# Later chunks: the values of the last two batches, between the fourth up quarter's products and its 64-row rest, in the accumulators' free columns set to zero

## The chip, the cores and the metric

The kernel runs on one core of one Trainium2 chip. The metric is device time in microseconds (us). The core has five engines that run their own instruction streams and wait for one another by semaphores: TensorE (PE; its weight loads are listed as PEld), VectorE (DVE), ScalarE (ACT), GpSimd (POOL) and SyncE (SP), whose queue here issues nearly all DMAs. Matmuls write to PSUM, which has eight banks of 512 float32 columns on 128 partitions.

## The reference

An mLSTM cell over 4 batches, 8 heads, 768 steps and head size 40 is followed by a feed-forward block with exact GELU on 3072 tokens (320 features, 2048 hidden). Cut to what matters:

```
for t in range(S):
    m_new = max(f[t] + m, i[t])
    C = exp(f[t] + m - m_new) * C + exp(i[t] - m_new) * outer(v[t], k[t])
    n = exp(f[t] + m - m_new) * n + exp(i[t] - m_new) * k[t]
    y[t] = sigmoid(o[t]) * (C @ q[t]) / max(abs(n @ q[t]), 1)
x = y as (tokens, heads * head size)
out = gelu(x @ w_in) @ w_out
```

## The kernel before

The sequence is cut into six chunks of 128 steps. In a chunk the cell is computed in parallel form: scores k q, masked and weighted by W, times the values v, plus what the state from earlier chunks gives ("far"). The feed-forward block of a chunk c runs on TensorE while the cell of chunk c + 1 is computed in between, so that each later chunk (1 to 5) is one long list of steps. Float32 accuracy comes from splitting each operand: x into x_hi, x_rest and x_low, the hidden values g into three parts, the weights into two, so each product is three passes.

The order of the steps is written out by hand in strings: SECOND for chunk 1, LATER for chunks 2 to 4, LAST for chunk 5. A word is a letter with its number, and each engine gets its instructions in the order of the words. A word that concerns one engine only can stand anywhere between words of other engines without a change. The words that matter here:

- U q, u q: the four up quarters. U is the products with K = 128 (24 matmuls of 512 columns, L966), u its rest with the last 64 rows of x (12 matmuls on half the array, L977). Quarter 0 writes the four banks called main, quarters 1 to 3 the four banks called side. side and main each are two pools with two banks; they change places from chunk to chunk. In a quarter the first 12 matmuls of U fill the two banks of the first pool, the other 12 those of the second.
- g n: gelu of one of 16 hidden blocks on ACT (L984), its first part on ACT (L985), the two others on DVE (L986, L987). The whole value lies in a tile with the tag "sig", of which there are two.
- d n: the down products of block n (L991, 12 matmuls of 320 columns) into the four accumulators po in main. An accumulator takes 320 of the 512 columns of its bank; the free ones are called beside.
- C b, h b: for the batches b and b + 1 the state is read (read_two, L621), then the update's products are made (L632), far is scaled on DVE (L639), the state is decayed on POOL (L643) and added to on DVE (L647). Both use two banks of side, called pf.
- S b: the scores of two batches (L568), in all four banks of side; DVE multiplies them into W (L574).
- V b: the values of one batch (later_values, L674, 32 small matmuls for a batch, two records each), added to far on DVE (L678). Batches 0 and 1 go to beside, 2 and 3 to a bank of side.
- Y b, t b, X b, R b: the output gate and the division on DVE (L685 to L690), a copy on ACT, the transposes on PE (L708) into a bank px of side, and the split into the parts of x on ACT (L718) and DVE (L727, L728).
- E t: the accumulators of the chunk before are copied to o_sb on ACT (L1015), two to a tile of the tag "o_sb", of which there are two, and sent by SP in two halves each (L859).
- K, Q: transposes of k and q on DVE (L512). D: values times a decay on POOL. M: masking of W on POOL (L474). W: its exponentials on ACT (L500). G: the output gate's tanh on ACT.
- L, B, J, O and +: loads and copies by SP's queue: blocks of k and q, M for W, k and v, the output gate, and copies of k and q in DRAM for later chunks.

In the code before, far has two buffers of its own (tag "hs"). far of batches 0 and 1 takes them in h0; when these batches are through X, far of batches 2 and 3 takes them in h2.

Of the kernel before, what the change touches and what calls it, by code (L numbers as in the profile page):

```python
# [9 lines left out]
F32 = mybir.dt.float32  # L10
# [4 lines left out]
OP = mybir.AluOpType  # L15

P = 128
# [18 lines left out]
for at, first, key in ((HI_AT, 10, "h0"), (LO_AT, 10, "h1"), (HI_AT, 13, "b0"), (LO_AT, 13, "b1"), (HI_AT, 0, "b2"), (LO_AT, 0, "b3")):  # L36
    at.update((first + i, (key, i)) for i in range(3))
LATER = """
 U0 u0 E0 E1 E2 E3 K1 Q1 L2 D0 D1 C0 h0 M2 M3 g0 g1 g2 g3 +
 U1 u1 g4 d0 g5 d1 g6 d2 g7 S0 d3 K2 Q2 L3 W2 W3 G0 G1 G2 G3 +  # L40
 U2 V0 V1 u2 g8 d4 g9 K3 Q3 B4 B5 J0 J1 d5 g10 d6 g11 S2 L4 d7
 U3 u3 + M4 M5 Y0 Y1 D2 D3 K4 W4 W5 g12 t0 d8 g13 t1 d9 g14 X0 X1 R0 d10 g15 R1 C2 h2 O0 O1 d11 V2 V3 Y2 t2 B6 J2 d12 Y3 t3 Q4 L5 B7 d13 X2 X3 R2 d14 R3 d15 + O2 O3"""

SECOND = """
 U0 u0 j2 o0 o1 K1 Q1 L2 M0 M1 D0 D1 W0 W1 a0,3 b0,3 a3 b3 a4,2 b4,2 a6,2 b6,2 C0 h0 M2 M3 g0 g1 g2 g3 o2 o3 + +
 U1 u1 Z Z Z g4 d0 g5 d1 g6 d2 g7 S0 d3 K2 Q2 L3 W2 W3 G0 G1 G2 G3 Z Z +
 U2 V0 V1 u2 + g8 d4 g9 K3 Q3 B4 B5 J0 J1 d5 g10 d6 g11 S2 L4 d7
 U3 u3 + M4 M5 Y0 Y1 D2 D3 K4 W4 W5 g12 t0 d8 g13 t1 d9 g14 X0 X1 R0 d10 g15 R1 C2 h2 O0 O1 d11 V2 V3 Y2 t2 B6 J2 d12 Y3 t3 Q4 L5 B7 d13 X2 X3 R2 d14 R3 d15 + O2 O3"""

LAST = """  # L50
 U0 u0 E0 E1 E2 E3 g0 g1 g2 g3 U1 u1 g4 d0 g5 d1 g6 d2 g7 d3 
# [5 lines left out]
def kernel(  # L57
# [16 lines left out]
    nc = tc.nc  # L74

    B, H, S, D = q.shape
    L = P
    NCH = S // L
    NP = H // 2
    D1 = D + 1  # L80
    DP = 64
    BH = B * H
    DM = H * D
    DFF = moe_w_in.shape[1]
    NF = DFF // P
    TG = B * L
# [13 lines left out]
    raw = ctx.enter_context(tc.tile_pool(name="raw", bufs=2))  # L100
    two = ctx.enter_context(tc.tile_pool(name="two", bufs=2))
    outp = ctx.enter_context(tc.tile_pool(name="outp", bufs=2))
    dram = ctx.enter_context(tc.tile_pool(name="dram", bufs=1, space=bass.MemoryType.DRAM))
    ps_tr = ctx.enter_context(tc.tile_pool(name="ps_tr", bufs=2, space=bass.MemoryType.PSUM))
    ps_h = ctx.enter_context(tc.tile_pool(name="ps_h", bufs=2, space=bass.MemoryType.PSUM))
    ps_mm = ctx.enter_context(tc.tile_pool(name="ps_mm", bufs=2, space=bass.MemoryType.PSUM))
# [25 lines left out]
    vb = [const.tile([P, H, D1], F32, name=f"vb{n}", tag=f"vb{n}") for n in range(NQ)]  # L132
# [29 lines left out]
    def load(n, first=0, end=4):  # L162

        if n >= NCH * B:
            return
        c, b = divmod(n, B)
        for src, dst in ((q, qb), (k, kb), (v, vb), (o_gate, None))[first:end]:
            if dst is kb and c > 1:
                dst = k_later
            if dst and swapped(c, b):  # L170
                x, to = src[b, :, c * L:(c + 1) * L, :].rearrange("h p d -> p h d"), dst[turn_of(n)][:, :, 0:D]
                for i in range(2):
                    nc.sync.dma_start(out=to[halves[i]], in_=x[halves[1 - i]])
                continue
            nc.sync.dma_start(out=dst[turn_of(n)][:, :, 0:D] if dst else out_of(n),
                              in_=src[b, :, c * L:(c + 1) * L, :].rearrange("h p d -> p h d"))
# [19 lines left out]
    def turn_of(n):  # L196

        return n % NLD if n < 2 * B else (n - 2 * B) % NQ
# [184 lines left out]
    bits, sig, pow2 = {}, {}, {}  # L383
# [46 lines left out]
    def unread(bank):  # L430
        for _ in range(idle[0]):
            nc.tensor.matmul(bank, ident, ident, start=True, stop=True, skip_group_check=True)
        idle[0] = 0

    def per_head(t, c, b):
        return t[:, c, b * H:(b + 1) * H].unsqueeze(2)
# [5 lines left out]
    def by_set(px):  # L442

        return px.rearrange("p k (a i) -> p (k a) i", a=2)

    def in_place(x, b):

        return x.rearrange("p k (a t) -> p (k a) t", a=2)[:, :, b * R:(b + 1) * R]
# [9 lines left out]
    class Cell:  # L458
# [153 lines left out]
        def read_two(self, b0):  # L612

            c, two_b = self.c, (b0, b0 + 1)
            banks = self.banks = [self.side[1][0].tile([P, H + NP, D1], F32, name="pf", tag=self.side[1][1]) for _ in range(2)]
            for i, b in enumerate(two_b):
                qT = self.qT[b]
                for p in range(NP):
                    for r in halves:
                        for hip in range(2):  # L620
                            nc.tensor.matmul(banks[hip][r, NP * i + p, :], qT[halves[hip], p, r],  # L621
                                             state[b][halves[hip], p, 0:D1], start=True, stop=True)

        def update_two(self, b0):

            c, two_b, banks = self.c, (b0, b0 + 1), self.banks
            if c + 1 < NCH:
                for i, b in enumerate(two_b):
                    vw = self.vw.pop(b)
                    for p in range(NP):  # L630
                        for hip in range(2):
                            nc.tensor.matmul(banks[i][used[hip], H + p, :], k_later[turn_of(c * B + b)][:, 2 * p + hip, :],  # L632
                                             vw[:, 2 * p + hip, :], start=True, stop=True)
            add = []
            for i, b in enumerate(two_b):
                self.far[b] = fars[0].tile([P, H, D1], F32, name="far", tag="hs", bufs=2)
                by_hip = lambda t, hip: t.rearrange("p (m two) d -> p m two d", two=2)[:, :, hip, :]
                for hip in range(2):
                    nc.vector.tensor_tensor(out=by_hip(self.far[b], hip), in0=banks[hip][:, NP * i:NP * i + NP, :],  # L639
                                            in1=by_hip(per_head(gT, c - 1, b), hip).to_broadcast([P, NP, D1]), op=OP.mult)  # L640
                if c + 1 < NCH:
                    st, d = state[b][:, :, 0:D1], dec[:, c - 1, b * NP:(b + 1) * NP].unsqueeze(2).to_broadcast([P, NP, D1])
                    nc.gpsimd.tensor_tensor(out=st, in0=st, in1=d, op=OP.mult)  # L643
                    for r in used:
                        add.append((st[r], banks[i][r, H:H + NP, :]))
            for st, to in add:
                nc.vector.tensor_tensor(out=st, in0=st, in1=to, op=OP.add)  # L647

# [11 lines left out]

        def later_values(self, b):

            n, hs = self.c * B + b, self.far.pop(b)
            Pm = W.pop(n)
            by_hip = lambda t: [t.rearrange("p (m two) d -> p m two d", two=2)[:, :, hip, :] for hip in range(2)]
            if b < 2:
                ph = beside[2 * b:2 * b + 2]
            else:
                whole = self.side[0][0].tile([P, H, D1], F32, name="ph", tag=self.side[0][1])
                ph = by_hip(whole)  # L670
            for hip in range(2):
                for p in range(NP):
                    for r in quarters:
                        nc.tensor.matmul(ph[hip][r, p, :], Pm[:, 2 * p + hip, r], vb[turn_of(n)][:, 2 * p + hip, :], start=b > 1,  # L674
                                         stop=True, skip_group_check=b < 2)
            self.hs[b] = hs
            for to, x in zip(by_hip(hs), ph) if b < 2 else ((hs, whole),):
                nc.vector.tensor_tensor(out=to, in0=x, in1=to, op=OP.add)  # L678

        def finish(self, b):  # L680
            n, hs = self.c * B + b, self.hs.pop(b)
# [18 lines left out]

        def turn_y(self, b):
            n, t = self.c * B + b, slice(b * L, (b + 1) * L)
            pool, tag = self.side[b // 2] if self.c > 1 else (ps_tr, "tr") if self.c > 0 else (ps_mm, "b")
            px = pool.tile([P, NX + 1, L], F32, name="px", tag=tag)
            unread(px[:, 0, :])
            for k in range(NX + 1):
                y = ob[n % NLD][:, k * P:(k + 1) * P] if k < NX else self.rest.get(b, y_rest).rearrange("p two r -> p (two r)")
                nc.tensor.transpose(px[:, k, :], y, ident)  # L708
            self.turned.append(b)
            if self.c < 2 and len(self.finished) > len(self.turned):  # L710
                self.twice(b + 1)
            if self.c == 0:
                nc.scalar.copy(out=first_x[:, :, t], in_=px)
                return
            self.px[b] = px
            if "x" not in parts:
                parts["x"] = raw.tile([P, NX + 1, TG], F32R, name="x_hi", tag="x", bufs=1)
            nc.scalar.activation(out=in_place(parts["x"], b), in_=by_set(px), func=AF.Copy, scale=PART)  # L718
            if self.c == 1 and b < 2:
                load(n + NLD, 1, 3)  # L720
# [12 lines left out]
    parts, fars, w_hi, w_lo, beside = {}, [], {}, {}, []  # L733
# [304 lines left out]
    def first_blocks():  # L1038
# [3 lines left out]
        for r in (32, 96):  # L1042
# [8 lines left out]
                 d=lambda: decays_last(0, 1), q=lambda: decays_last(1, NCH - 1), r=halves_out, p=halves_back,  # L1051
# [56 lines left out]
```

## Time and profile before

| | us |
|---|---|
| median of 3 runs | 438.81 |
| lowest and highest of them | 438.38, 438.86 |
| the profiled execution, its own time | 438.46 |
| its span | 436.7 |
| granted TensorE clock | 1.0 |

The profile follows one execution. Its page gives the busy time of each engine; the chain of waits is the chain of work that ended last, followed back from the last instruction; the timeline gives each engine's instructions in order of time. Where a row has "[idle before <-releaser]", the engine stood idle for that long, and what is named ended it. The rows of the SyncE queue (SPq) are issues of DMAs; "to landing" counts from an issue until the data has arrived. The page's groups for the work around the change, with count, busy time and mean of one:

```profile
L986 DVE TENSOR_TENSOR g_parts<-g_whole,g_parts 128x512 fp32r<-128x512 f32 x80 | 57.0, 713 | 58.1 <-ACT g_parts L985 56.0
L984 ACT ACTIVATE g_whole<-pu 128x512 f32<-128x512 f32 x80 | 47.1, 589 | 74.2 <-PE pu L977 63.7
L574 DVE TENSOR_TENSOR W<-ps,W 128x256 f32<-128x256 f32 (+1 forms) x48 | 17.7, 414 | 4.2 <-PE ps L568 3.2
out_dram<-o_sb SPq DMA_DIRECT2D x36, 80.0 KB, 2.0
```

### The profile page before, as it was taken

The numbers are of one execution on the slowest core, as the hardware profiler recorded it, in microseconds if no ns is written. First come the engines' busy times: TensorE is split into PE (matmuls) and PEld (weight loads), VectorE is DVE, ScalarE is ACT, GpSimd is POOL, SyncE is SP. The second block draws the span as 40 slices with busy tenths as digits, with TensorE's granted clock in tenths as the row PEclk, the third lists the DMA queues.
The fourth block names the chain that finished last, engine by engine and source line by source line (L and its number), as shares of the span: only waits on it lengthen the run. The fifth ranks groups of instructions, "written<-read, shape, count | busy, mean of one in ns | idle before, by whom it ended". The sixth has DMA issues, their size and how long they took to land.

```text
span 436.7 us, 13291 instructions
## 1 busy us (share of the span) xinstructions
PE 427.3 (98%) x5472; PEld 374.6 (86%) x5472; DVE 296.0 (68%) x680; ACT 277.3 (63%) x595; POOL 48.8 (11%) x77
## 2 busy tenths in 40 slices
PE   8989999999999999999999999999999999999996
PEld 7777888877988899988899988899988889979986
DVE  8797687797888697747597747597746586533330
ACT  4989999856889985228785229785247715243441
POOL 3001030000430041030041030040010000000000
PEclk9999999999999999999999999999999999999999
DMA  7999994577791592662492653571561400010001
GB/s 151 220 214 243 233 256 87 138 211 179 229 154 56 106 176 60 115 179 50 84 187 42 123 158 60 117 134 32 110 156 17 62 2 2 22 42 2 1 2 60
DMA packets 162268, 48.83 MB, mean 112 GB/s; under 512 B 147776, under 2 KB 155232, under 8 KB 162208
## 3 DMA queue, kind: packets, MB, share of 16 engines
q1 hardware_dynamic: 161888, 47.65, 50.1%
q8 instruction: 43, 0.70, 0.6%
q10 hardware_dynamic: 320, 0.33, 0.2%
q14 instruction: 17, 0.14, 0.1%
HBM read 43.84 MB, written 9.37 MB: 122 GB/s over the span
## 4 chain that ended last, share of the span: by engine, by line
PE 73%; DVE 2%; ACT 2%; DMA 1%; issue 1%; ACTq 0%
PE po L991 31%; PE pu L966 24%; PE pu L977 7%; PE ps L568 3%; PE pf L621 2%; PE ph L674 1%; PE po L888 1%; PE po L674 1%; PE px L708 1%; DMA bits<-in_moe_w_out_dram 1%; PE pf L632 1%; DVE pow L416 1%; DVE w_out L419 0%; ACT w_out_part L935 0%; ACT g_part L873 0%
## 5 line engine op out<-in xcount | busy, mean ns | idle before, releaser
L991 PE MATMUL po<-w_out_part,g_parts 128*128 128x320 f32 x960 | 140.7, 303 | 0.0
L991 PEld LDWEIGHTS po<-w_out_part,g_parts 128*128 128x128 f32 x960 | 131.6, 189 | 5.9 <-issue 4.6
L986 DVE TENSOR_TENSOR g_parts<-g_whole,g_parts 128x512 fp32r<-128x512 f32 x80 | 57.0, 713 | 58.1 <-ACT g_parts L985 56.0
L984 ACT ACTIVATE g_whole<-pu 128x512 f32<-128x512 f32 x80 | 47.1, 589 | 74.2 <-PE pu L977 63.7
L985 ACT ACTIVATE g_parts<-g_whole 128x512 fp32r<-128x512 f32 x80 | 50.5, 631 | 8.3 <-PE po L991 5.1
L474 POOL TENSOR_SCALAR_AFFINE_SELECT W<-W 128x1024 f32<-128x1024 f32 (+2 forms) x20 | 21.7, 1088 | 189.2 <-DMA W<-M_d 154.4
L500 ACT ACTIVATE W<-W,aT 128x128 f32<-128x128 f32 x128 | 38.8, 389 | 0.3
L987 DVE CAST g_parts<-g_whole 128x512 fp32r<-128x512 f32 x80 | 36.2, 453 | 0.0
L699 ACT COPY far<-ob 128x128 f32<-128x128 f32 x16 | 4.6, 290 | 32.9 <-DVE ob L690 32.9
L966 PE MATMUL pu<-x_hi,w_in_hi 128*128 128x512 f32 x80 | 24.2, 384 | 0.0
L966 PE MATMUL pu<-x_hi,hi_first 128*128 128x512 f32 x80 | 24.0, 381 | 0.1
L966 PE MATMUL pu<-x_rest,hi_first 128*128 128x512 f32 x80 | 23.8, 379 | 0.0
L966 PE MATMUL pu<-x_rest,w_in_hi 128*128 128x512 f32 x80 | 23.8, 379 | 0.0
L966 PE MATMUL pu<-x_low,w_in_lo 128*128 128x512 f32 x80 | 23.8, 379 | 0.0
L966 PE MATMUL pu<-x_low,w_in 128*128 128x512 f32 x80 | 23.8, 379 | 0.0
L888 PE MATMUL po<-w_out,g 128*128 128x320 f32 x80 | 22.0, 432 | 0.0
L404 ACT ACTIVATE sig<-bits 128x320 f32<-128x320 f32 (+1 forms) x26 | 15.2, 586 | 10.4 <-issue 6.1
L574 DVE TENSOR_TENSOR W<-ps,W 128x256 f32<-128x256 f32 (+1 forms) x48 | 17.7, 414 | 4.2 <-PE ps L568 3.2
L888 PEld LDWEIGHTS po<-w_out,g 128*128 128x128 f32 x80 | 15.0, 190 | 5.9
L639 DVE TENSOR_TENSOR far<-pf,gT 128x164 f32<-128x164 f32 x32 | 8.4, 319 | 16.1 <-PE pf L632 11.7
L416 DVE SCALAR_TENSOR_TENSOR pow<-sig,pow 128x320 uint32<-128x320 uint32 (+1 forms) x26 | 15.4, 592 | 4.3 <-ACT pow L405 4.3
L1015 ACT ACTIVATE o_sb<-po 128x320 f32<-128x320 f32 x20 | 7.5, 443 | 16.7 <-PE po L991 16.7
(196 smaller groups left out, 778.9 us busy)
## 6 DMA issues: line engine op xcount, KB each, us to landing
W<-M_d SPq DMA_DIRECT2D x16, 512.0 KB, 6.5
bits<-in_moe_w_in_dram SPq DMA_DIRECT2D x20, 256.0 KB, 4.2
bits<-in_moe_w_out_dram SPq DMA_DIRECT2D x16, 320.0 KB, 4.6
blocks<-kq_d SPq DMA_DIRECT2D x32, 128.0 KB, 3.5
ob<-in_o_gate_dram SPq DMA_DIRECT2D x24, 160.0 KB, 4.1
out_dram<-o_sb SPq DMA_DIRECT2D x36, 80.0 KB, 2.0
wide<-M_d SPq DMA_DIRECT2D x4, 512.0 KB, 4.8
kq_d<-in_k_dram SPq DMA_DIRECT2D x6, 320.0 KB, 4.6
```

The source lines that it names most:

```text
L416: nc.vector.scalar_tensor_tensor(out=p, in0=s, scalar=3, in1=p, op0=OP.logical_shift_left, op1=OP.bitwise_or)
L474: nc.gpsimd.affine_select(out=x, in_=x, compare_op=OP.is_ge, fill=1.0e30, base=base, pattern=[[0, H], [1, x.shape[2]]], channel_multiplier=-1)
L500: nc.scalar.activation(out=W[n][:, h, :], in_=src, func=AF.Exp, scale=-1.0, bias=aT[:, self.c, r:r + 1])
L574: nc.vector.tensor_tensor(out=w[r, :, t], in0=ps[i][hip][r, :, t], in1=w[r, :, t], op=OP.mult)
L888: nc.tensor.matmul(to, xs[k][:, b * L:(b + 1) * L], w, start=(n == 0 and k == 0), stop=(n == NF - 1 and k + 1 == len(xs)), skip_group_chec ...
L966: nc.tensor.matmul(in_pairs(pus[i][e]), w3(at[k])[n][:, e, i * P:(i + 1) * P], in_turns(x3[n][:, k, :]), start=(n == 0 and k == 0), stop=F ...
L977: nc.tensor.matmul(in_pairs(pus[i][e]), w3(r)[n][h, p % 2, i * P:(i + 1) * P], in_turns(x3[n][h, NX, :]), start=False, stop=(n == 2), skip ...
L984: nc.scalar.activation(out=whole, in_=self.pus[n // 4][n % 4 // 2][n % 2], func=AF.Gelu)
L985: nc.scalar.activation(out=hi, in_=whole, func=AF.Copy, scale=PART)
L986: nc.vector.tensor_tensor(out=rest, in0=whole, in1=hi, op=OP.subtract)
L987: nc.vector.tensor_copy(out=low, in_=whole)
L991: nc.tensor.matmul(in_pairs(self.po[t]), x[:, t * L:(t + 1) * L], in_turns(w), start=(n == 0 and k == 0), stop=(n == NF - 1 and k == 2), s ...
```

## The change

The order of the steps changes in LATER, and in SECOND from the third up quarter on. TensorE's order in a later chunk is, with the down products:

```
before  U0 u0 C0 h0 U1 u1 d0-d2 S0 d3 U2 V0 V1 u2 d4-d6 S2 d7 U3 u3 d8 d9 X0 X1 d10 C2 h2 d11 V2 V3 d12 d13 X2 X3 d14 d15
after   U0 C0 u0 h0 U1 u1 d0-d2 S0 d3 U2 V0 V1 u2 d4-d6 S2 d7 U3 V2 V3 u3 d8 d9 C2 h2 X0 d10 X1 d11 d12 X2 d13 d14 X3 d15
```

In SECOND, C0 stays behind u0. Words of other engines move with these (K3 and Q3 on DVE come around g8 instead of behind g9, M3 on POOL comes ahead of D0 in LATER, M5 and W5 ahead of M4 and W4, t0 and t1 ahead of g12, Y2 ahead of g15, one more copy step in LATER). The code:

- V2 and V3 use beside too. After V1's additions, DVE sets the four free parts to zero, and the matmuls of V2 and V3 add to them. Their results are copied to two tiles of the tag "hs", which only batches 2 and 3 use now.
- far of batches 0 and 1 lies in the tiles of the tag "o_sb"; far of batches 2 and 3 in tiles of the tag "sig", and it is added to the copied values in h2.
- The banks of side that pf and px take are exchanged for batches 2 and 3, and 0 and 1.

```diff
         def read_two(self, b0):
-            banks = self.banks = [self.side[1][0].tile([P, H + NP, D1], F32, name="pf", tag=self.side[1][1]) for _ in range(2)]
+            pool, tag = self.side[0 if b0 else 1]
+            banks = self.banks = [pool.tile([P, H + NP, D1], F32, name="pf", tag=tag) for _ in range(2)]
...
-                self.far[b] = fars[0].tile([P, H, D1], F32, name="far", tag="hs", bufs=2)
+                self.far[b] = (raw.tile([P, TG], F32, name="far", tag="sig") if b0 else
+                               outp.tile([P, 2, DM], F32, name="far", tag="o_sb").rearrange("p two d -> p (two d)"))[:, 0:H * D1].rearrange(
+                                   "p (h d) -> p h d", d=D1)
...
+            for b in two_b if b0 else ():
+                hs = self.hs[b]
+                nc.vector.tensor_tensor(out=hs, in0=self.far.pop(b), in1=hs, op=OP.add)
...
         def later_values(self, b):
-            n, hs = self.c * B + b, self.far.pop(b)
+            n = self.c * B + b
+            hs = self.hs[b] = self.far.pop(b) if b < 2 else fars[0].tile([P, H, D1], F32, name="hs", tag="hs", bufs=2)
...
-            if b < 2:
-                ph = beside[2 * b:2 * b + 2]
-            else:
-                whole = self.side[0][0].tile([P, H, D1], F32, name="ph", tag=self.side[0][1])
-                ph = by_hip(whole)
+            ph = beside[b % 2 * 2:b % 2 * 2 + 2]
...
+                    nc.vector.tensor_copy(out=to, in_=x)
+            if b == 1:
+                for x in beside:
+                    nc.vector.memset(x, 0.0)
...
         def turn_y(self, b):
-            pool, tag = self.side[b // 2] if self.c > 1 else (ps_tr, "tr") if self.c > 0 else (ps_mm, "b")
+            pool, tag = self.side[1 - b // 2] if self.c > 1 else (ps_tr, "tr") if self.c > 0 else (ps_mm, "b")
```

More of the change, by code (lines that the diff above doesn't have):

```diff
@@ L38 @@
 LATER = """
[L39 to L42, printed above, removed]
+ E0 U0 E1 E2 K1 Q1 E3 L2 D1 C0 M3 u0 D0 h0 g0 g1 g2 g3 M2 U1 u1 g4 + d0 d1 g5 g6 d2 g7 S0 d3 K2 Q2 L3 G2 W2 W3 G3 G1 G0
+ + U2 V0 V1 u2 d4 K3 g8 Q3 B4 B5 g9 d5 J0 J1 g10 d6 g11 S2 L4 d7 U3 M5 Y0 M4 W5 W4 t0 Y1 t1 V2 V3 K4 u3 D3 D2 g12 d8 + g13
+ d9 g14 C2 h2 X0 d10 Y2 g15 X1 t2 Y3 t3 Q4 d11 R0 R1 d12 O0 O1 X2 d13 R2 B6 J2 d14 X3 R3 L5 B7 + O2 O3 d15"""
 SECOND = """
[L45 to L48, printed above, removed]
+ U0 u0 j2 o0 o1 K1 Q1 L2 M0 M1 D0 D1 W0 W1 a0,3 b0,3 a3 b3 a4,2 b4,2 a6,2 b6,2 C0 h0 M2 M3 g0 g1 g2 g3 o2 o3 + + U1 u1 Z Z Z g4
+ d0 g5 d1 g6 d2 g7 S0 d3 K2 Q2 L3 W2 W3 G0 G1 G2 G3 Z Z + U2 V0 V1 u2 + d4 K3 g8 Q3 B4 B5 g9 d5 J0 J1 g10 d6 g11 S2 L4
+ d7 U3 M5 Y0 M4 W5 W4 t0 Y1 t1 V2 V3 K4 u3 D3 D2 g12 d8 + g13 d9 g14 C2 h2 X0 d10 Y2 g15 X1 t2 Y3 t3 Q4 d11 R0 R1 d12 O0 O1 X2
+ d13 R2 B6 J2 d14 X3 R3 L5 B7 + O2 O3 d15"""
 LAST = """
@@ L673, in later_values @@
                     for r in quarters:
[L674 to L678, printed above, removed]
+                        nc.tensor.matmul(ph[hip][r, p, :], Pm[:, 2 * p + hip, r], vb[turn_of(n)][:, 2 * p + hip, :], start=False,
+                                         stop=True, skip_group_check=True)
+            for to, x in zip(by_hip(hs), ph):
+                if b < 2:
+                    nc.vector.tensor_tensor(out=to, in0=x, in1=to, op=OP.add)
+                else:
+                    nc.vector.tensor_copy(out=to, in_=x)
+            if b == 1:
+                for x in beside:
+                    nc.vector.memset(x, 0.0)
         def finish(self, b):
```

## The prediction, made before the changed kernel ran

> **What bounds the kernel now.** I read the page first, then the chain of waits in order of time, then the timeline of the engines that must feed TensorE.
>
> ```profile
> span 436.7 us, 13291 instructions
> PE 427.3 (98%) x5472; PEld 374.6 (86%) x5472; DVE 296.0 (68%) x680; ACT 277.3 (63%) x595; POOL 48.8 (11%) x77
> ```
>
> TensorE (PE) has 9.4 us without work in the whole span. So the change can win only by making a stretch of matmuls shorter, and it loses as soon as one matmul has to wait. Each row of the chain of waits has a start, a duration, the engine, tile and line, and a count. This is chunk 3 from its first up quarter (U0), with the values step of chunk 1 behind it:
>
> ```profile
> 249.96 5.18 PE pu L966 x24
> ...
> 256.63 1.07 PE pf L621 x64
> 257.70 0.74 PE pf L632 x32
> 258.44 5.38 PE pu L966 x24
> ...
> 273.73 5.18 PE pu L966 x24
> 278.91 1.38 PE po L674 x119
> 280.29 1.49 PE pu L977 x12
> 281.78 5.09 PE po L991 x36
> ...
> 295.71 1.49 PE pu L977 x12
> 297.20 3.46 PE po L991 x24
> 300.66 0.65 PE px L708 x6
> 301.32 1.63 PE po L991 x12
> 302.95 1.07 PE pf L621 x64
> 304.02 0.74 PE pf L632 x32
> 304.77 1.83 PE po L991 x12
> 306.59 1.50 PE ph L674 x114
> 308.09 3.46 PE po L991 x24
> 311.55 0.71 PE px L708 x6
> 312.26 3.26 PE po L991 x24
> ```
>
> ```profile
> 175.22 1.48 PE ph L674 x120
> 176.69 0.35 issue
> ```
>
> PE never leaves the chain. The same work has two prices, by what stands ahead of it. Twelve down products (L991) cost 1.63 behind transposes, 1.83 behind the small matmuls of L632, and 3.46 is 1.83 + 1.63. An up quarter (L966, 24 matmuls) costs 5.18 behind down products and 5.38 behind L632. So entering full tiles from small ones costs 0.20. The values step (L674) costs 1.38 between U2 and its rest, and 1.50 between down products, with 0.20 more on the products behind it.
>
> **The change part by part.** *PE.* Taking V2 V3 from between the products to between U3 and u3 replaces 1.50 + 0.20 by 1.38, and the rest still costs 1.49 (280.29, where it stands behind a values step already). The entry price behind h2 stays; transposes X0 pay it now. The transposes cost the same one by one, 0.11 each (0.65 / 6). In full, from 295.71: 1.38 + 1.49 + 3.46 + 1.07 + 0.74 + (0.33 + 0.20) + 1.63 + 0.33 + 3.26 + 0.35 + 3.26 + 0.35 + 1.63 = 19.48, where before it is 19.81: a gain of 0.33 in each of four chunks, 1.3. In chunk 1 the values step also had a gap of 0.35 that no wait explains; the new place may have it too, so I count half: 0.2. PE gains 1.5, bounds 1.2 and 2.0. C0 ahead of the rest u0, in place of behind it, leaves as many entries as before: nothing.
>
> [...]
>
> *VectorE (DVE), clearing.* Four memsets of 128x164 in PSUM stand behind the additions of V0 V1, and the products d4, which write the same banks, wait for them.
>
> ```profile
> 279.41 1.36 DVE L678 TENSOR_TENSOR far<-po,far 128x164 f32<-128x164 f32 x4 [3.06 <-PE po L674]
> 258.18 1.11 DVE L639 TENSOR_TENSOR far<-pf,gT 128x164 f32<-128x164 f32 x4 [5.44 <-PE pf L632]
> 259.21 1.34 DVE L647 TENSOR_TENSOR state<-state,pf 40x164 f32<-40x164 f32 x4
> 307.56 1.09 DVE L678 TENSOR_TENSOR far<-ph,far 128x328 f32<-128x328 f32 x2
> 290.73 1.78 DVE L574 TENSOR_TENSOR wide<-ps,wide 128x256 f32<-128x256 f32 x4
> ```
>
> The trace has no memset in PSUM. The nearest rows are 128x164 operations on PSUM at 0.26 each (four from 258.18 to 259.21) to 0.34 (1.36 / 4); the other bound is nothing. I take 0.26, by the row that writes without adding: they end at 280.77 + 1.04 = 281.81, while d4 starts at 281.78 and reaches the fourth bank three products, 0.42, later. At 0.34 they end at 282.13, still ahead of 282.20. Without that cover each memset would cost PE its 0.26. [...]
>
> V2 needs W of batches 2 and 3: finished at 292.51 (290.73 + 1.78), while U3 ends at 295.71, so V2 waits for nothing. The copies out of the banks are covered by u3 (1.49).
>
> *The new home of far 0 and 1.* This is the step that I expect to decide. far of batches 0 and 1 moves from its own buffers to the two o_sb buffers, and these are being sent to DRAM just then: E0 to E3 fill them at the start of the chunk, and h0 writes far there on DVE. So DVE now waits in h0 for the output DMAs. The next fence has the eight sends of chunk 3 in SyncE's queue, the last three of them (issue and landing); the one behind it the last sends of chunks 2 and 4, the starts of their U1, and, at 245.90, what releases the loads that stand ahead in the queue.
>
> ```profile
> 252.20 8.37 SPq L859 DMA_DIRECT2D out_dram<-o_sb  x8
> ...
> L859 SPq DMA_DIRECT2D out_dram<-o_sb x3: 546/587/587, 258.7 to 260.0; - x3
> DMA to landing us min/median/max: 2.0/2.0/2.0
> ```
>
> ```profile
> L859 SPq DMA_DIRECT2D out_dram<-o_sb x3: 587/591/936, 192.0 to 193.6; - x3
> L859 SPq DMA_DIRECT2D out_dram<-o_sb x1: 587/587/587, 323.7 to 323.7; - x1
> 193.21 5.38 PE pu L966 x24
> 323.26 5.38 PE pu L966 x24
> 320.18 1.80 POOL L474 TENSOR_SCALAR_AFFINE_SELECT wide<-wide 64x1024 f32<-64x1024 f32 x2 [7.49 <-DMA wide<-M_d]
> 245.90 0.70 DVE L512 STREAM_TRANSPOSE qT<-blocks 128x512 f32<-128x512 f32 x1
> 246.63 2.27 SPq L191 DMA_DIRECT2D blocks<-kq_d  x4
> ```
>
> In chunk 3 the last send is issued at 260.0 and lands at 262.0, while far starts at 258.18 today. Queued on DVE behind far 1 are the four state additions and the splits of g0 and g1. Waiting for the additions is PE: far and the additions read the banks of pf, and these are the third and fourth bank that U1 writes, from its 13th matmul on. That matmul is due 0.20 + 12 x 0.216 = 2.79 after U1's start: 261.2 before, 260.9 after 0.33 gained. The queue will run somewhat earlier, because its block loads are released by the transpose at 245.90, which stands behind h2 on DVE, and h2 comes earlier (C2 at 302.04 in place of 302.95, worked out under X1); the x splits of batch 1, ahead of it today, move behind it too. I take 0.6, bounds 0 and 1.4. Then the last landing is 261.4; far 1 takes 0.52, the first state pair 0.67, handovers some 0.2: the bank is free at 262.8, 1.9 after it is due. By the same reckoning chunk 2: landing 193.6 + 2.0 - 0.6 = 195.0, bank free at 196.4, due at 193.21 + 2.79 less 0.33 to 0.7, so 195.4: 1.0. Chunk 4 has no state update: landing 325.1, far's first half done by 325.6, due at 325.7: nothing. Sum 2.9; with the queue 1.4 earlier 1.1, with it unmoved and the landing 0.6 slower about 4.7. Chunk 1 finds chunk 0's output in o_sb, which was sent ahead of U0: I take nothing. The splits of g0 to g7, behind it on DVE, come late too, but PE by then as well.
>
> *POOL.* Mask M3 now stands ahead of D0, and h0 waits for D0. Chunk 4 shows when M3 can run: its load lands 4.66 after U0's start at 315.52, and it ends at 6.46. D0 is a product of 128x328, under 1 by the DVE row of that size, so done by 7.5; h0 is due at 5.18 + 1.07 + 1.49 = 7.74. Cover holds by 0.2; a load 1 us later would cost PE 0.8 in chunks 2 and 3.
>
> *X1.* far 2 and 3 take turns with g_whole, so gelu 15 must wait for far 2 to be added, and X1 needs the bank that gelu 15 reads.
>
> ```profile
> 296.59 0.60 ACT L984 ACTIVATE g_whole<-pu 128x512 f32<-128x512 f32 x1 [2.68 <-PE pu L977]
> 299.91 0.63 ACT L985 ACTIVATE g_parts<-g_whole 128x512 fp32r<-128x512 f32 x1
> ```
>
> With V first, the rest ends at 298.58, the products d8 d9 at 302.04, and X1 is due after another 1.07 + 0.74 + 0.53 + 1.63, at 306.01. ACT is done with g14 at 299.91 + 0.63 today, 1.38 later then, 301.92, early enough for DVE's part of it. far starts 1.55 after C2 (as in h0, 256.63 to 258.18), 303.59; four of them end at 304.70, the addition takes 0.55 (1.09 / 2), gelu 15 0.60, two handovers some 0.2: 306.05. So 0.1 in each of chunks 1 to 3, bounds 0 and 0.4. In chunk 4 PE has no L632 (0.74) ahead of X1, and DVE gains less: 0.35. Sum 0.65, bounds 0 and 1.6. The other moves on ACT (masks' exponentials in another order, t0 and t1 ahead of g12) lie in its idle 2.68 ahead of g12, which the values step ahead of u3 makes longer by 1.38.
>
> Sum: -1.5 + 2.9 + 0.65 = +2.05. The profiled execution has 438.46, 0.35 under the median of 438.81, so the sum gives 440.5 on its own time and 440.9 on the median. I say 440.5, the lower, because the size of the largest term is the least sure.
>
> **The rivals.** (1) *Faster: the sends land in time.* Should the queue be free some 2 us earlier, DVE never waits at far 1, and what is left is -1.5 + 0.65, or -1.5 if X1 is free too: 437.0 to 437.6. For it: eight sends at 0.59 would take 4.7 of the 8.37, so the queue stands for 3.7 behind transfers that came first, and these are in another order after the change. Against it: the loads ahead are the same bytes and are issued no more than about 1 us earlier. With a landing at 259.5 in chunk 3 (the due time 260.9 less 1.4) nothing is left of the wait. (2) *No change:* the sends come 0.7 earlier than I take them, the waits at U1 are half, 1.4, and the sum is +0.55: 439.0. (3) *Worse:* the sends leave no earlier and land 0.6 slower, as under a fuller queue: 4.7 in place of 2.9, 442.3. Against it: h2, which releases the loads ahead, does come earlier. (4) *The change doesn't do what it says:* V2 waits for W at U3's end, as a new stall in all four chunks; the 3.2 us between 292.51 and 295.71 speak against it.
>
> **How the numbers follow.** About 0.2% (0.9 us) is what a measurement of this kernel can tell from no change. Forecast 0.55, rival 1 0.13, rival 2 0.20, rival 3 0.10, rival 4 0.02. Slower by over 0.2% (above 439.7) holds the forecast, rivals 3 and 4: 0.67; within: 0.20; faster: 0.13. The range 437.9 to 442.3 leaves out most of rival 1 and the top of rival 3.
>
> **What would show it.** In the chain of waits: L676 behind U3 at 1.4, and products at 1.63 where 1.83 stood. On DVE: idle time ahead of the second far of h0 (L641), ended by an out_dram DMA, about 3 us in chunk 3. On PE: idle time in the middle of U1 (L973), ended by DVE state, in chunks 2 and 3 and not in 4. At X1 (L715): a wait for gelu, largest in chunk 4. The prediction is wrong if far isn't held by the sends, or if U1's third bank is free by the time it is due.

## The result and the profile after

| | before | after |
|---|---|---|
| median, us | 438.37 (16 runs) | 440.62 (16 runs) |
| lowest and highest, us | 436.52, 440.08 | 439.14, 443.99 |
| the profiled execution, its own time, us | 438.46 | 440.29 |
| its span, us | 436.7 | 438.5 |

The ratio of after to before is 1.0061, 95% interval 1.0046 to 1.0077: the changed kernel is slower by 0.6%, 2.7 us of 438.4, with an interval from 2.0 to 3.4. The ratio is not that of the two medians, which differ by 2.25. The profiled executions differ by 1.83.

The page of the changed kernel, its span, its engines, and the group of the far products on DVE (count, busy time and mean of one, then idle time ahead of them and what ended most of it):

```profile
span 438.5 us, 13285 instructions
...
PE 426.9 (97%) x5472; PEld 374.3 (85%) x5472; DVE 302.9 (69%) x712; ACT 278.9 (64%) x595; POOL 49.0 (11%) x77
...
L641 DVE TENSOR_TENSOR far<-pf,gT 128x164 f32<-128x164 f32 x32 | 8.6, 321 | 23.2 <-DMA out_dram<-o_sb 18.9
```

TensorE's busy time fell by 0.4 and the span grew by 1.8. So the work did not become dearer; PE waits more. The last row names whom DVE waits for: 18.9 us ahead of far, ended by the output DMAs. Most of that costs nothing, because DVE, busy for 69% of the span where PE is busy for 97%, is not the engine that bounds the kernel. What reaches PE stands in the view of PE's waits of the changed kernel (total, how often, longest):

```profile
PE pu L973 <- DVE state L652: 2.6, 2, 1.7
```

Both are in U1. The timeline of DVE at far 1 in h0 of chunks 2 and 3, and behind it PE's two matmuls that waited, of the changed kernel:

```profile
196.07 0.56 DVE L641 TENSOR_TENSOR far<-pf,gT 128x164 f32<-128x164 f32 x2 [1.72 <-DMA out_dram<-o_sb]
...
262.36 0.56 DVE L641 TENSOR_TENSOR far<-pf,gT 128x164 f32<-128x164 f32 x2 [2.00 <-DMA out_dram<-o_sb]
262.84 1.34 DVE L652 TENSOR_TENSOR state<-state,pf 40x164 f32<-40x164 f32 x4
```

```profile
197.35 0.67 PE L973 MATMUL pu<-x_hi,w_in_hi 128*128 128x512 f32 x2 [1.73 <-DVE state L652]
...
263.63 0.67 PE L973 MATMUL pu<-x_hi,w_in_hi 128*128 128x512 f32 x2 [0.92 <-DVE state L652]
```

The chain of waits of the changed kernel in chunk 3 links them: last output send, far 1, the first two state additions, the second half of U1.

```profile
251.44 5.18 PE pu L973 x24
...
260.27 1.97 DMA out_dram<-o_sb
...
262.36 0.56 DVE far L641 x2
262.92 0.22 DVE state L652
...
263.16 0.34 DVE state L652
...
263.63 2.83 PE pu L973 x12
...
276.37 5.18 PE pu L973 x24
...
298.10 1.38 PE po L676 x121
```

From U0 to U2 chunk 3 takes 276.37 - 251.44 = 24.93, where before it took 273.73 - 249.96 = 23.77: 1.16 more. In chunk 2 the same stretch grew by 1.96 (U0 at 184.35, U2 at 210.08; before 184.72 and 208.49), and not in chunk 4. Together that is 3.12, of which 2.65 is the wait itself (1.73 and 0.92) and 0.48 the restart, 0.24 each time (2.83 for 12 matmuls that take 2.59 in a row). The last row is the moved values step: 1.38, straight behind U3, with no wait. It takes 1.38 in chunk 4 too, 1.49 in chunk 1 and 1.47 in chunk 2.

The gain is there too. From U3 to the next U0 the four later chunks took 25.56, 25.00, 25.23 and 24.38 before, and take 24.79, 24.89, 24.63 and 24.12 now: 1.74 less. That sum still contains the waits at X1. The chain of chunk 4, where they are largest, of the changed kernel:

```profile
368.62 1.14 PE pf L621 x64
369.76 1.02 DVE far L641 x4
370.78 0.42 DVE hs L650
...
371.22 0.61 ACT g_whole L991
...
371.87 0.55 PE px L715 x3
```

So the time was lost in one place: the output sends, which now hold DVE in h0. One piece of the 1.83 is hardly the change's: chunk 1 began 0.38 later (119.23 against 118.85), in a stretch that the change does not touch. In the other kernels here it began at 118.16 to 120.77.

### The profile page after: what moved, and what is told of

The parts are those of the page before. It is cut to its first block, busy times and chain, and to the rows that moved or that the text cites. A ratio compares the mean times of both kernels' runs of the same rounds, so it can differ in the third digit from the quotient of the medians.

```text
span 438.5 us, 13285 instructions
## 1 busy us (share of the span) xinstructions
PE 426.9 (97%) x5472; PEld 374.3 (85%) x5472; DVE 302.9 (69%) x712; ACT 278.9 (64%) x595; POOL 49.0 (11%) x77
## 4 chain that ended last, share of the span: by engine, by line
PE 70%; DVE 3%; ACT 3%; DMA 2%; issue 1%; SPq 0%; DVEq 0%; ACTq 0%
PE po L998 30%; PE pu L973 23%; PE pu L984 7%; PE ps L567 3%; PE po L676 3%; PE pf L621 2%; PE po L895 1%; PE px L715 1%; DMA bits<-in_moe_w_out_dram 1%; DMA out_dram<-o_sb 1%; PE pf L632 1%; ACT g_whole L991 1%; DVE far L641 0%; ACT w_out_part L942 0%; DVE pow L415 0%
## 5 line engine op out<-in xcount | busy, mean ns | idle before, releaser
L993 DVE TENSOR_TENSOR g_parts<-g_whole,g_parts 128x512 fp32r<-128x512 f32 x80 | 55.4, 693 | 46.8 <-ACT g_parts L992 44.5
L994 DVE CAST g_parts<-g_whole 128x512 fp32r<-128x512 f32 x80 | 34.1, 427 | 0.0
L641 DVE TENSOR_TENSOR far<-pf,gT 128x164 f32<-128x164 f32 x32 | 8.6, 321 | 23.2 <-DMA out_dram<-o_sb 18.9
L725 ACT ACTIVATE x_hi<-px 128x384 fp32r<-128x384 f32 x20 | 9.8, 488 | 18.1 <-PE px L715 18.1
L973 PEld LDWEIGHTS pu<-x_hi,w_in_hi 128*128 128x128 f32 x80 | 14.3, 189 | 5.7 <-issue 4.1
```

The source lines that it names most:

```text
L973: nc.tensor.matmul(in_pairs(pus[i][e]), w3(at[k])[n][:, e, i * P:(i + 1) * P], in_turns(x3[n][:, k, :]), start=(n == 0 and k == 0), stop=F ...
L993: nc.vector.tensor_tensor(out=rest, in0=whole, in1=hi, op=OP.subtract)
L994: nc.vector.tensor_copy(out=low, in_=whole)
```

## Experiments

Times are compared with runs of the kernel before on the same chip: medians of 438.85 for the first four kernels, 439.22 for the last four. A difference between two kernels measured on different chips is taken from their ratios. The numbers in brackets behind a ratio are its 95% interval. The expectations are written on the scale of runs that were known by then, in part from another chip, so they are compared as differences; s1 and s2 in them are experiments 2 and 3. U0 to U0 means the time from U0 of chunk 1 to U0 of chunk 5 in a trace.

**1. far of batches 0 and 1 in o_sb, alone, in the kernel before.** Theory: the new home is the whole loss. Rival: the loss comes from the new order of the steps.

```diff
-                self.far[b] = fars[0].tile([P, H, D1], F32, name="far", tag="hs", bufs=2)
+                self.far[b] = (fars[0].tile([P, H, D1], F32, name="far", tag="hs", bufs=2) if b0 else
+                               outp.tile([P, 2, DM], F32, name="far", tag="o_sb").rearrange("p two d -> p (two d)")[:, 0:H * D1].rearrange(
+                                   "p (h d) -> p h d", d=D1))
```

> The kernel before, with one part of the change alone: far of batches 0 and 1 lies in the o_sb buffers. Order, values and banks are those of before. Theory (far waits for the output's landing, and U1's third bank for far and the state additions): U1 waits in chunk 2 from 195.99 to about 197.3 and in chunk 3 from 261.2 to about 263.4, nearly nothing in chunk 4; with some 0.2 for starting again each time +3.5 to +4.2 us: 442.0 to 442.6. Rival A (the loss of the changed kernel comes from its added DVE work or its order of steps, not from this buffer): no change, 438.4.

Measured: 443.26 (6 runs), ratio 1.0110 [1.0078, 1.0142]. PE's waits of this kernel:

```profile
PE pu L968 <- DVE state L649: 3.9, 2, 2.0
```

The one edit gives the wait of the changed kernel, and a larger loss than the whole change: about 1.1% against 0.6%. So the home alone is enough for the loss; that the new order has no part in it is for experiment 2 to show. The four runs whose mean granted clock was not below 0.999 have a median of 442.7, 3.8 above the kernel before, within what was expected. The other two are slower still, as told under what was not expected. One part of the theory missed: in chunk 4, where nearly nothing was expected, U1 waited 0.38 for far, and the stretch from U0 to U2 grew by 0.62.

**2. The changed kernel with two homes exchanged.** Batches 0 and 1 keep the buffers of the kernel before (tag "hs"), and the copies of the values of batches 2 and 3 go to o_sb, which is free by then. No memory is added. Theory: the U1 waits vanish and PE's gain stays. Rival: the copies meet the sends as well.

```diff
-                self.far[b] = (raw.tile([P, TG], F32, name="far", tag="sig") if b0 else
-                               outp.tile([P, 2, DM], F32, name="far", tag="o_sb").rearrange("p two d -> p (two d)"))[:, 0:H * D1].rearrange(
-                                   "p (h d) -> p h d", d=D1)
+                self.far[b] = (raw.tile([P, TG], F32, name="far", tag="sig")[:, 0:H * D1].rearrange("p (h d) -> p h d", d=D1) if b0 else
+                               fars[0].tile([P, H, D1], F32, name="far", tag="hs", bufs=2))
...
-            hs = self.hs[b] = self.far.pop(b) if b < 2 else fars[0].tile([P, H, D1], F32, name="hs", tag="hs", bufs=2)
+            hs = self.hs[b] = self.far.pop(b) if b < 2 else outp.tile([P, 2, DM], F32, name="hs", tag="o_sb").rearrange("p two d -> p (two d)")[:, 0:H * D1].rearrange("p (h d) -> p h d", d=D1)
```

> The changed kernel with two buffers exchanged: far of batches 0 and 1 in the tiles 'hs', the copied values of batches 2 and 3 in the tiles 'o_sb' (the output that was in them landed some 40 us earlier). Order and amount of work are the same. Theory: the waits in U1 (1.73 and 0.92 in the trace of the changed kernel, 3.1 with the restart) go, nothing else moves: 440.6 - 3.1 = 437.5, some 0.9 under the kernel before. Rival A: as the changed kernel, 440.6. Rival B (DVE is short of time there anyway, and the wait only moves to the scores): 439 to 440.

Measured: 436.61 (12 runs), ratio 0.9966 [0.9946, 0.9985]: faster than the kernel before, by 1.5 where some 0.9 was expected; the interval reaches about 0.8 to either side. By the traces U0 to U0 is 3.47 shorter than in the changed kernel, where 3.1 was expected: 3.11 of it lies from U0 to U2, and 0.30 behind U3, nearly all in chunk 2, where X1 waits less and the values step takes 1.38 in place of 1.47. The chain of waits of this kernel has U1 of chunks 2 and 3 whole again:

```profile
193.56 5.38 PE pu L972 x24
...
258.42 5.38 PE pu L972 x24
```

From U0 of chunk 1 to U0 of chunk 5 it takes 258.53, the changed kernel 262.00, the kernel before 260.54. With the new order kept, the home alone decides between a gain of 2.0 and a loss of 1.5.

**3. Experiment 2 with X1 behind d11.** It tests whether the waits at X1 are time lost. Both order strings change alike:

```diff
- d9 g14 C2 h2 X0 d10 Y2 g15 X1 t2 Y3 t3 Q4 d11 R0 R1 d12
+ d9 g14 C2 h2 X0 d10 Y2 g15 d11 X1 t2 Y3 t3 Q4 R0 R1 d12
```

> As s1, and X1 behind d11 in place of ahead of it, so that gelu 15 has 1.63 us more before X1 needs its bank. Theory: the waits at X1 (0.09 + 0.22 + 0.04 in chunks 1 to 3, 0.29 in chunk 4, by the trace of the changed kernel) go, 0.6 less than s1: 436.9. Rival: DVE reaches the last x split as late as before or later, and U0 of the next chunk waits: as s1 or up to 0.5 above it.

Measured: 437.44 (12 runs), ratio 0.9980 [0.9962, 0.9998]: it cannot be told apart from experiment 2, so the expected 0.6 is not seen. The waits at X1 are gone, but a new one stands in PE's waits. The second fence has the matmuls of chunk 3 that waited, from the chain of this kernel:

```profile
PE pf L632 <- POOL vw L538: 0.7, 2, 0.5
```

```profile
256.12 0.75 POOL vw L538
...
256.91 0.81 PE pf L632 x32
```

This is M3 ahead of D0 on POOL: a load for M3 that lands late makes D0 late, and with it h0 (in chunk 3 the load landed at 254.09 in this kernel's chain, and D0 began at 256.12, behind two masks). The prediction gave that cover 0.2 us; here it did not hold. Why the load landed later here, no run shows.

**4. The changed kernel with the sends put ahead in SyncE's queue.** far stays in o_sb. The two loads of the output gate (O2 O3) and one copy step (+) move from the end of a chunk to behind the next chunk's sends; o2 and o3 are the same loads, named from the chunk that follows. Theory: the landing is set by when the sends are issued. Rival: it is set by the bytes in flight, and this gains nothing.

```diff
- E0 U0 E1 E2 K1 Q1 E3 L2 D1 C0 M3
+ E0 U0 E1 E2 K1 Q1 E3 + o2 o3 L2 D1 C0 M3
...
- d13 R2 B6 J2 d14 X3 R3 L5 B7 + O2 O3 d15
+ d13 R2 B6 J2 d14 X3 R3 L5 B7 d15
```

> The changed kernel with the last copy step and the output gate loads O2 O3 of a chunk moved in SyncE's queue behind the eight sends at the start of the next chunk. Buffers as in the changed kernel. Theory: the sends start some 2.5 us earlier (the three issues that stood ahead: 251.44 instead of 253.37 at the earliest in chunk 3, then 0.59 each, less of them blocked) and land 2 us behind the last issue, by about 258.5 in chunk 3; U1's waits go down to 0 to 0.5: 437.5 to 438. Rival C (the landing is set by the bytes already queued, not by the issue): landing stays near 262, 440 to 440.6.

Measured: 437.1 (8 runs), ratio 0.9957 [0.9939, 0.9975]. One of the eight took 2261.8 us, for a reason that nothing here shows, and is not in the ratio; the other seven lie between 435.69 and 437.56, with a median of 436.77. By the ratio that is 1.9 under the kernel before, where the expected 437.5 to 438 meant 0.4 to 0.9. The sends of chunks 2 and 3 in SyncE's queue, first of the changed kernel, then of this one:

```profile
186.08 8.50 SPq L866 DMA_DIRECT2D out_dram<-o_sb  x8
...
253.37 7.49 SPq L866 DMA_DIRECT2D out_dram<-o_sb  x8
```

```profile
185.17 5.06 SPq L866 DMA_DIRECT2D out_dram<-o_sb  x8
...
249.85 5.57 SPq L866 DMA_DIRECT2D out_dram<-o_sb  x8
```

Counted from U0 the sends of chunk 3 are all issued after 9.42 in the changed kernel (U0 at 251.44) and after 5.67 here (U0 at 249.75). They begin 1.83 earlier, and the issues themselves are shorter by 1.92. U1 is whole in both chunks, by the chain of this kernel:

```profile
193.38 5.38 PE pu L973 x24
...
258.24 5.38 PE pu L973 x24
```

So the place in the queue decides: with three transfers taken from ahead of the sends, the home does no harm. The edit makes the sends start earlier and their issues shorter at once; it does not separate the two. In chunk 2 U1 starts 0.14 later, because D0 stands behind M3 on POOL as in experiment 3.

**5. Experiment 2 with V2 V3 between d8 and d9.** It puts the values step back between products, which tests where PE's gain comes from. In both order strings:

```diff
- t1 V2 V3 K4 u3 D3 D2 g12 d8 + g13
+ t1 K4 u3 D3 D2 g12 d8 V2 V3 + g13
```

> As s1, and V2 V3 behind d8 in place of ahead of u3; nothing else is moved. It prices the place. Theory (rows: 1.38 ahead of the rest against 1.50 and 0.20 on the product behind it): 4 x 0.33 = 1.3 above s1, 437.9, and in the chain the values at 1.5 with d9 at 1.83. [...] Rival (the place is worth nothing): as s1, 436.6.

Measured: 440.48 (12 runs), ratio 1.0024 [1.0008, 1.0041]; against experiment 2, 0.58% (0.32 to 0.84 when the two half-widths are added in squares), 2.5 us, and 2.45 by the traces from U0 of chunk 1 to U0 of chunk 5. That is more than the 1.3 expected, and not the rival's nothing. The chain in chunk 1, and what waited in chunks 2 and 3, of this kernel:

```profile
168.59 1.50 PE po L675 x121
170.09 1.93 PE po L997 x12
```

```profile
235.50 2.19 PE L997 MATMUL po<-w_out_part,g_parts 128*128 128x320 f32 x12 [0.25 <-DVE hs L681]
...
301.29 2.19 PE L997 MATMUL po<-w_out_part,g_parts 128*128 128x320 f32 x12 [0.30 <-DVE hs L681]
```

Where nothing waits, the step and the products behind it (1.50 + 1.93) cost 0.42 more than 1.38 + 1.63, not 0.33. (Chunk 1 itself loses only 0.28, because there the step takes 1.52 in experiment 2.) In chunks 2 and 3 a wait is added that the expectation did not have: d9 writes the banks that the values are being copied out of, and those copies stand behind the split of g12 on DVE. In experiment 2 the rest u3, which uses other banks, covers them. So the place between U3 and u3 is worth two things, the price of the step and the cover of its copies.

**6. Experiment 3 with D0 ahead of M3.** It takes D0 out from behind the thin cover that experiment 3 laid open; M3 comes behind h0's decay of the state on POOL. In the order of chunks 2 to 4:

```diff
- L2 D1 C0 M3 u0 D0 h0 g0
+ L2 D1 D0 C0 u0 h0 M3 g0
```

> As s2, and D0 ahead of mask M3 on POOL. In s2 the products of h0 waited for D0, which stood behind M3, which waited for its load (0.5 and 0.2 in chunks 2 and 3). Theory: these 0.7 go and X1 stays free of its wait, so the gain of both is seen: 0.6 under s1 and 0.7 under s2, 436.0, with no wait of PE over 0.1 in chunks 1 to 4. Rival: the masks come too late for the exponentials W3 then, and the scores wait: 437 or more.

Measured: 437.29 (11 runs), ratio 0.9946 [0.9929, 0.9963]. No wait of PE over 0.1 us is left in the later chunks, and U0 to U0 takes 258.05, the shortest of all. By the trace that is 0.48 under experiment 2, where 0.6 was expected. It beats the kernel before and the changed kernel. Its interval overlaps with those of experiments 2 and 4, so which of the three is fastest is open. Its tail of chunk 3, from the values step, shows PE's gain without any wait:

```profile
296.01 1.38 PE po L675 x120
297.39 1.49 PE pu L983 x12
298.88 3.46 PE po L997 x24
...
304.15 0.48 PE px L714 x3
...
307.89 0.33 PE px L714 x3
```

**7. Experiment 2 with the four memsets three times.** It takes away the cover that the memsets were said to have.

```diff
-                for x in beside:
+                for x in beside * 3:
```

> As s1, with each of the four memsets done three times. It prices the cover of the memsets. In s1, chunk 2, the four take 0.73 from 215.81 and the products d4 start at 216.82. Theory (d4 waits for them, bank by bank): twelve end at 217.4 to 218.0 and d4 waits about 0.75, in four chunks +3.0: 439.6, and up to 1.5 more if the late gelu 10 and 11 then hold the scores S2. Rival (columns that the products don't write hold nothing back): as s1, 436.6.

Measured: 441.17 (12 runs), ratio 1.0047 [1.0028, 1.0065]; 0.81% above experiment 2 (0.53 to 1.09, in the same way), 3.6 us, within what was expected. PE's waits and, behind them, the memsets in the chain of chunk 2, of this kernel; last the memsets of experiment 2 on DVE's timeline:

```profile
PE po L997 <- DVE po L684: 3.1, 4, 1.1
```

```profile
216.96 1.63 DVE po L684 x9
...
218.63 5.28 PE po L997 x36
```

```profile
215.81 0.73 DVE L684 MEMSET po<- 128x164 f32 x4
```

In experiment 2 the memsets end at 216.54 and d4 starts at 216.89 in its chain: covered by 0.35. With eight more, d4 waits for the ninth, the last one on its first bank. Five memsets of 0.18 less the 0.35 of cover are 0.55; in chunk 2 d4 waits 0.60, and its products take 5.28 in place of 5.09. So here the memsets ahead of a bank's products cost PE, behind the cover, about their length: 0.60 for 0.55.

**8. Experiment 2 with C0 behind u0.**

```diff
- L2 D1 C0 M3 u0 D0 h0 g0
+ L2 D1 u0 C0 M3 D0 h0 g0
```

> As s1, with C0 behind the rest u0 in chunks 2 to 4, as before the change. Theory: it costs and brings nothing, 436.6 within 0.5, with C0 at 1.07 and h0 at 0.74 in the chain in both places. Rival: its new place brings part of the gain, 0.2 a chunk: 437.2 or more.

Measured: 437.64 (12 runs), ratio 0.9960 [0.9939, 0.9981], the same as experiment 2 within the intervals. U0 to U0 takes 258.45 against 258.53. The place of C0 is worth nothing that these runs can see.

Not tried: far in buffers of its own. Whether the core's memory has room for them beside the tiles of this kernel, no run shows.

## Why the prediction was right, step by step

The prediction of 440.5 was a sum on the profiled execution's own time, 438.46 + 2.05. That execution has 440.29 now, 1.83 more, and the median is 440.62. The mechanism was right. PE's term was sized too small, and the parts of the largest term, far, were off in opposite directions.

| step | predicted, us | measured, us |
|---|---|---|
| PE: values step moved | -1.5 | -2.38 |
| far 0 and 1 held by the output sends | +2.9 | +3.12 |
| X1 held by gelu 15 | +0.65 | +0.64 |
| memsets, copies, V2's wait for W, C0, POOL | 0 | 0 |
| chunk 1 begins later | not in it | +0.38 |
| sum | +2.05 | +1.76 |

The 0.07 between 1.76 and 1.83 is left over in small pieces (from U2 to U3 the four chunks take 0.08 more).

- **PE's gain was mis-sized.** The tails lost 1.74 with 0.64 of X1 waits in them: 2.38. Experiment 6, without these waits, gives 24.69, 24.57, 24.57 and 23.83: 2.51 below the kernel before, outside the bounds of 1.2 to 2.0. Each tail gains 0.42, not 0.33: three transposes cost 0.33, and 0.48 behind L632, where the sum had 0.35 twice and 0.53 (fence of experiment 6). That is 0.4 over four chunks. The gap in chunk 1 was counted half, 0.2; without it chunk 1 gains 0.45 on top of the 0.42. The rest is 0.24 in U3 of chunk 3 and 0.13 in the values step of chunk 4: both were slower in the one profile of before (5.42 for U3, a step in two pieces), for a reason that the trace does not give, so this 0.37 need not be the change's.
- **Where a tail's 0.42 comes from.** By the chains of chunk 3, before and in experiment 6, the products take 0.40 less (13.24 against 13.64: twice 1.63 in place of 1.83), the values step 0.12 less (1.38 against 1.50), and the transposes 0.11 more (0.48 and three times 0.33 against 0.65 and 0.71). Four times 0.42, with the 0.45 of the gap in chunk 1 and the 0.37 just named, is 2.50 of the 2.51.
- **far held by the sends was the deciding step**, as predicted, by the chain that was predicted, with DVE's idle time ahead of far 1 at 1.72 and 2.00. For chunk 3 the prediction had said about 3: it had far 0 start without a wait, but far 0 waits for the sends too (DVE stood idle for 4.57 ahead of it and began it at 259.80). Its parts were off by 0.7 to 1.0 in opposite directions: chunk 2 predicted 1.0 and measured 1.96, chunk 3 predicted 1.9 and measured 1.16. The queue came earlier by 0.3 in both, not 0.6 (the sends begin 1.73 and 1.93 after U0, where they began 1.99 and 2.24). And the eight sends took 8.50 in chunk 2 where they had taken 7.53, and 7.49 in chunk 3 where they had taken 8.37. Why the sends were longer in one chunk and shorter in the other, no run here shows. That the sum came out so near is in part luck: the two chunks' errors cancel, and the late start of chunk 1 (+0.38) makes up for part of PE's larger gain.
- **X1** was right in size and in place: in the chain X1 takes 0.42, 0.55 and 0.37 in chunks 1 to 3 in place of 0.33, so 0.09, 0.22 and 0.04, and the tail of chunk 4 is 0.29 longer than in experiment 6 (24.12 against 23.83); predicted were 0.1, 0.1, 0.1 and 0.35. Experiment 3 shows that they can be removed.
- **Memsets** took 0.195 each, not 0.26, and were covered as argued; experiment 7 shows the price without cover. The group of these memsets in the changed kernel (shortest, median and longest, ns):

```profile
L685 DVE MEMSET po<- x16: 195/195/195, 150.4 to 348.1; 128x164 f32 x16
```
- **The rivals.** The first, that the sends land in time, does not happen in the changed kernel. Experiments 2 and 4 make it happen by other means. By U0 to U0 they are 2.0 and 1.8 below the kernel before (258.53 and 258.70 against 260.54), so 436.5 and 436.6 on its 438.46, where the rival's price was 437.0 to 437.6; that was a little too high, because PE's gain was put too low. The second and third would have waits at U1 of 1.4 and 4.7; the trace has 3.12. V2 does not wait for W. POOL's cover held in the changed kernel (no wait at L632 in its view) and broke in experiment 3.

## What to carry to other kernels

A buffer whose last use is a store was free here only when the store had landed (in chunk 3 of the changed kernel the last send landed at 262.24 and far 1 began at 262.36): look up when its sends are issued in their queue, and what stands behind the new tenant's first write. When a change both wins and loses, look for another pairing of the same buffers: here the exchange of two homes, with no memory added, turned a loss of 0.6% into a gain of 0.3%. Here a step stayed hidden only by its cover, so write each cover down with its size; the two thin ones (0.2 us on POOL, 0.35 at the memsets) came through in experiments 3 and 7.

## What the runs showed of the hardware that was not expected

In experiment 1 the profiled execution has a stretch with a lower granted clock, down to 0.50, just behind its second wait in U1. That the wait caused it, no run shows. The stretches of that kernel (from and to, length, busy time of PE, PEld, DVE, ACT and POOL with the count of instructions, granted clock, DMA share and rate):

```profile
120.00:260.00 140.00, 137.60 (x1884) 122.40 (x1882) 100.63 (x227) 88.49 (x193) 22.63 (x30) 1.00 0.57 114
...
266.00:268.00 2.00, 1.29 (x4) 1.10 (x5) 1.91 (x6) 0.00 (x0) 0.00 (x0) 0.76 0.97 108
268.00:270.00 2.00, 2.00 (x7) 1.53 (x6) 1.56 (x4) 1.56 (x3) 0.00 (x0) 0.50 0.78 175
270.00:272.00 2.00, 2.00 (x13) 1.47 (x13) 1.76 (x4) 0.79 (x2) 0.00 (x0) 0.89 0.01 4
```

```profile
266.71 4.51 PE pu L968 x12
```

```profile
199.36 0.67 PE L968 MATMUL pu<-x_hi,w_in_hi 128*128 128x512 f32 x2 [2.04 <-DVE state L649]
266.71 0.88 PE L968 MATMUL pu<-x_hi,w_in_hi 128*128 128x512 f32 x2 [1.90 <-DVE state L649]
```

The second half of U1 takes 4.51 in place of 2.83, 1.7 us on top of a wait of 1.90. By the last three rows of the stretches the clock fell short of full by 0.48 + 1.00 + 0.22 = 1.70 us (an estimate: 2.00 times what 0.76, 0.50 and 0.89 lack to 1), the same 1.7. Over this execution the mean granted clock is 0.996. Of the runs here it was that low in 4 of 16 of the changed kernel (441.51 to 443.99; the other twelve have a median of 440.4) and in 2 of 6 of experiment 1, and in none of the other kernels' or of the kernel before. Both kernels with it have a wait of 1.7 us or more in U1; experiment 7, whose longest is 1.1, never shows it. Against it: the first wait of the same execution was longer, 2.04, and the clock stayed at 1.00 behind it, as it did behind the 1.73 of the changed kernel's trace. So such a wait is not enough by itself. That it has a part in it is the author's guess from the order and the counts; no run was made for it, and which wait came ahead of the drop in the executions without a trace is not known.
